# A third buffer for a pair's keys and values, and one normalising product a pair, in a kernel of attention and two expert layers

## The chip, the cores and the metric

The kernel runs on one core of a Trainium2 chip. The metric is the device time of one execution in microseconds, as the median of several runs. Beside the runs there is one profiled execution, from which all rows below come; its times count from the start of its span.

## The reference

Three layers follow each other. Only the first is touched by the change.

```python
# attention: 2 batches, 8 heads, 768 positions, 64 columns a head; 8 global keys, window of 96
scores = scale * np.matmul(q, k.transpose(0, 1, 3, 2))
is_global = pos[None, :] < n_global
is_local = (rel >= 0) & (rel < n_local)
keep = is_global | is_local
dist = np.where(is_global & ~is_local, n_local, np.abs(rel))
scores = scores - slopes[:, None, None] * dist
scores = np.where(keep, scores, -1e9)
a = np.exp(scores - np.max(scores, axis=-1, keepdims=True))
a = a / (np.sum(a, axis=-1, keepdims=True) + 1e-09)
x = np.matmul(a, v)                       # heads side by side: 1536 tokens x 512

# gated layer, 512 -> 1536 -> 512
xn = x / np.sqrt(np.mean(x * x, -1) + 1e-6) * rms_g
x = (silu(xn @ w_gate) * (xn @ w_val)) @ w_out

# 8 experts, each token goes to its best one
for e in range(8):
    out[mask_e] = gate[mask_e] * (np.maximum(x[mask_e] @ w1[e], 0) @ w2[e])
```

## The kernel before

The 1536 tokens are cut into six stages of two tiles of 128 (three stages a batch), and the heads into four pairs. A pair of heads in a stage is numbered 0 to 23 in the order of the work, four to a stage; one tile of 128 queries of such a pair is a unit, 0 to 47, so that pair 9 has the units 18 and 19. Because the window is shorter than a tile, a query tile needs its own key tile, the one before it and 32 columns of global keys.

`load_pair` (L200 on) brings a pair's keys, queries and values with DMAs of the SyncE queue. For the first eight pairs, called raw, keys and queries are used as they are, in float32: the matrix products of the scores (L533, L537, L538) read the loaded tiles `kn` and `qn` directly. For the later pairs `prep` splits them into a high and a low half: ScalarE writes the high half of the keys (L486, tile `kt`) and of the queries (L498, tile `qt`), GpSimd the low half of the keys (L489) and VectorE that of the queries (L499); the scores (L550) read `kt` and `qt`, so that `kn` and `qn` are free when these four have run. GpSimd also sets two columns of ones in the values' tile `vn` (L432), so that the product with the values gives the sums of the softmax as well, and copies windows of keys and values (L421, tiles `kt`, `vx`).

The first four pairs lie in tiles of their own (`duo`). From pair 4 on the three loaded tiles come from the pool `attn`, two buffers for each of `kn`, `qn` and `vn`. `prep(4)` and later ones also issue the loads of the pair two further on; `prep` of a pair stands in the code one pair ahead of its first unit, where the loop over units calls it.

A unit runs in three steps, `scores`, `turn` two units later and `values` three units after that. In `scores` TensorE writes the scores, VectorE adds the mask and takes the extreme (L557), ScalarE takes the exponential (L561). In `turn` TensorE transposes the probabilities into the PSUM banks `pt` (L572) and ScalarE copies them out (L580, tile `ptS`). In `values` TensorE multiplies them by the values (L601) into the one PSUM bank `xp`; after a pair's second tile VectorE takes the reciprocals of the sums (L608, L609) and scales both tiles into `duo` (L611).

When a stage's four pairs are done, `tail` normalises its rows and turns them (L387 to L404), and the gated layer can begin for it (`moe_block`, L769 on). In the first 60 us nothing else than attention and filling products (`warm`, L180) is there for TensorE; from then on products of the gated layer run between those of attention, until attention ends near 171 us. Weights of that layer are loaded and split at the same time (`convert64`, L334 to L354).

The order of instructions on each engine is drawn at build time by a planner: it has the program's order as priorities, a model of the durations, and the rule that a tile's buffer can be given out again when all readers of its last use are through. Each engine then runs its own list in order, and waits where it must. A change in the number of buffers therefore changes the list of every engine.

The lines of the loads ahead and of the buffers:

```python
nxt = range(NFP, NFP + 2) if gi == 0 else range(gi + 2, gi + 3) if gi >= NFP else ()
for gn in nxt:
    nat = [pool.tile([P, 2 * STAGE if x == "q" else 2 * DM if x == "k" else (ST_MAX + 1) * VW], F32, tag=f"{x}n", bufs=2, name=f"{x}n") for x in "kqv"]
    loaded.append(load_pair(*order[gn], *nat))
```

Of the kernel before, what the change touches and what calls it, by code (L numbers as in the profile page):

```python
# [8 lines left out]
F32 = mybir.dt.float32  # L9
# [5 lines left out]
ALU = mybir.AluOpType  # L15
# [4 lines left out]
P = 128  # L20
B, H, S, D = 2, 8, 768, 64
NT, DM, DFF = B * S, H * D, 1536
# [7 lines left out]
STARTS = [sum(SIZES[:i]) for i in range(len(SIZES))]  # L30
NSTAGE = len(SIZES)
ST = ST_MAX = max(SIZES)
STAGE = ST * P
TB = S // P
VW = 2 * (D + 1)
# [10 lines left out]
def kernel(  # L46
# [16 lines left out]
    nc = tc.nc  # L63
    slope = [2.0 ** (-(h + 1)) for h in range(H)]
    NFP, LATE = 4, 8
    NRAWG = 8
    XT = "ccccss"
    RING = "ccceewweec"
# [50 lines left out]
        out=nval, in0=nneg, scalar=4294967296.0, in1=nf[:, :, 0], op0=ALU.mult, op1=ALU.add  # L119
# [7 lines left out]
        out=flagf[:, 2:3], in0=nval[0:1, 1:2], scalar=float(LMAX), in1=flagf[:, 1:2], op0=ALU.is_le, op1=ALU.mult  # L127
# [11 lines left out]
        out=tri_f, in_=tri_f, pattern=[[1, P]], compare_op=ALU.is_gt, fill=0.0, base=0, channel_multiplier=-1  # L139
# [59 lines left out]
    def is_raw(st, hp):  # L199
        return st * NP + hp < NRAWG  # L200

    def load_pair(st, hp, kn, qn, vn):
        b, t0, nt = STARTS[st] // TB, STARTS[st] % TB, SIZES[st]
        i0 = 0 if t0 else 1
        nk = nt + 1 - i0
        k0 = (t0 - 1 + i0) * P
        hd = slice(P * hp, P * (hp + 1))
        if is_raw(st, hp):
            nc.sync.dma_start(out=kn[:, 0:nk * P], in_=kT[b][hd, k0:k0 + nk * P])
            nc.sync.dma_start(out=qn[:, 0:nt * P], in_=qT[b][hd, t0 * P:(t0 + nt) * P])  # L210
            nc.sync.dma_start(
                out=rows_of(vn)[:, i0:i0 + nk, 1:P + 1],
                in_=v[b, k0:k0 + nk * P, hd].rearrange("(t p) c -> p t c", p=P),
            )
            return kn, qn, vn
        for x, src in ((kn[:, 0:2 * nk * P], kT[b][hd, k0:k0 + nk * P]), (qn[:, 0:2 * nt * P], qT[b][hd, t0 * P:(t0 + nt) * P])):
            for r in range(2):
                nc.sync.dma_start(
                    out=x[D * r:D * (r + 1), :].rearrange("d (j s) -> d j s", j=2),
                    in_=src.rearrange("(j d) s -> d j s", j=2),  # L220
                )
        nc.sync.dma_start(
            out=rows_of(vn)[:, i0:i0 + nk, 1:P + 1],
            in_=v[b, k0:k0 + nk * P, hd].rearrange("(t p) c -> p t c", p=P),
        )
        return kn, qn, vn
# [7 lines left out]
    duo = [rp.tile([P, 2, DM], F32, name=f"duo{i}") for i in range(TT // 2)]  # L234
    part = [duo[i // 2][:, i % 2] for i in range(TT)]
# [54 lines left out]
    def body(is_fast):  # L290
# [9 lines left out]
        def ps(tag, bufs, name):  # L300
            return psum.tile([P, 512], F32, tag=tag, bufs=bufs, name=name)
# [108 lines left out]
        def fast_attention(pool):  # L410
            kg = pool.tile([P, NP, 2, GW], F32R, name="kg")

            kgr = pool.tile([P, NP, GW], F32, name="kgr") if NRAWG > NP else None
            kgn = pool.tile([P, NP, 2, GW], F32, name="kgn")
# [8 lines left out]
            def prep(gi):  # L423
                st, hp = order[gi]
                t0, nt = STARTS[st] % TB, SIZES[st]
                i0 = 0 if t0 else 1
                n = nt * P
# [6 lines left out]
                for gn in nxt:  # L434
                    if gn >= len(order):
                        break
                    nat = [
                        pool.tile([P, 2 * STAGE if x == "q" else 2 * DM if x == "k" else (ST_MAX + 1) * VW], F32, tag=f"{x}n", bufs=2, name=f"{x}n") for x in "kqv"
                    ]
                    loaded.append(load_pair(*order[gn], *nat))  # L440
                nk = nt + 1 - i0
                if gi == 0:
                    kg0 = kT[0].rearrange("(h d) s -> d h s", d=D)[:, :, 0:GW]
                    for r in range(2):
                        nc.sync.dma_start(
                            out=kgn[D * r:D * (r + 1)].rearrange("d a j s -> d (a j) s"), in_=kg0
# [3 lines left out]
                if gi == 2:  # L450
                    nc.scalar.activation(out=kg, in_=kgn, func=ACTF.Copy)
                    nc.gpsimd.tensor_tensor(
                        out=kg[D:P], in0=kgn[D:P], in1=kg[D:P].bitcast(F32), op=ALU.subtract
# [4 lines left out]
                f = 1 if t0 >= 2 else 3 - t0  # L458
# [34 lines left out]
                if hi_dve[1]:  # L493
                    nc.vector.tensor_scalar(
                        out=qhi, in0=srq, scalar1=0.125 / slope[2 * hp], scalar2=None, op0=ALU.mult
                    )
                else:
                    nc.scalar.activation(out=qhi, in_=srq, func=ACTF.Copy, scale=0.125 / slope[2 * hp])  # L498
                lo_eng[kq[1]].scalar_tensor_tensor(  # L499
                    out=qt[:, :, 1, 0:n], in0=srq, scalar=0.125 / slope[2 * hp], in1=qhi.bitcast(F32),  # L500
# [84 lines left out]
            def values(g, t, ptf, nb):  # L585
                st, t0, hp, qt, kt, vn, vx, mx = groups[g]
                nt = SIZES[st]
                if t == 0:
                    xps[g] = ps("x", 1, "xp")
                xp = xps[g]  # L590
                for j in range(2):
                    c = slice(j * (D + 1), (j + 1) * (D + 1))
                    o = xp[:, t * VW + j * (D + 1):t * VW + (j + 1) * (D + 1)]
                    for a in range(nb):
                        if nb == 1 or a == 1:
                            rhs = vn[:, t + 1, c]
                        elif t0 + t == 1:
                            rhs = vn[:, t, c]
                        else:
                            rhs = vx[:, t, c]  # L600
                        nc.tensor.matmul(  # L601
                            out=o, lhsT=ptf[:, (j * nb + a) * P:(j * nb + a + 1) * P], rhs=rhs,
                            start=(a == 0), stop=(a == nb - 1),
                        )
                if t == nt - 1:
                    rc = pool.tile([P, ST, 2], F32, tag="rc", bufs=2, name="rc")
                    xs3 = xp[:, 0:nt * VW].rearrange("p (t c) -> p t c", c=VW)
                    nc.vector.tensor_scalar(out=rc[:, 0:nt], in0=xs3[:, :, 0:VW:VW - 1], scalar1=1e-9, scalar2=None, op0=ALU.add)  # L608
                    nc.vector.reciprocal(rc[:, 0:nt], rc[:, 0:nt])  # L609
                    for tt in range(nt):  # L610
                        nc.vector.tensor_tensor(  # L611
                            out=part[STARTS[st] + tt][:, hp * P:(hp + 1) * P].rearrange("p (j d) -> p j d", j=2),
                            in0=xp[:, tt * VW + 1:tt * VW + 1 + P].rearrange("p (j d) -> p j d", j=2),
                            in1=rc[:, tt].unsqueeze(2).to_broadcast([P, 2, D]), op=ALU.mult,
                        )
                    groups[g] = None

            warm(WARM1)
            prep(0)
            yield "work"  # L620
            tails = []
            q1, q2 = [], []
            n = hold = 0
            while n < len(units) or q1 or q2:
# [18 lines left out]
                if last is not None:  # L643
                    g, t = last
                    if t == SIZES[g // NP] - 1 and g % NP == NP - 1:
                        st = g // NP
# [518 lines left out]
        while True:  # L1165
# [12 lines left out]
            while True:  # L1178
                if moe is None and ready:
                    st = ready.pop(0)  # L1180
# [45 lines left out]
        for a in range(KD):  # L1226
            raw = rp.tile([P, P, NE], F32, tag="raw", bufs=NRAW, name="rawg")
            nc.sync.dma_start(out=raw, in_=r_gate[a * P:(a + 1) * P, :].partition_broadcast(P))
            for h in range(2):
                nc.scalar.activation(  # L1230
                    out=rgb[h][:, :, a * P:(a + 1) * P],
# [34 lines left out]
        st, ms = NSTAGE - 1, range(M1, NM)  # L1266
        prep_next(0, first, len(first))
        banks["mm"] = MMC.split()
        with tc.manual_schedule(engines={mybir.EngineType.PE}):
# [10 lines left out]
            x = expert_tile(w1t[0], w2t[0], tka, wta, xsa, lambda: None, True)  # L1280
# [21 lines left out]
        for e in range(NE):  # L1302
# [17 lines left out]
            if e == 0:  # L1320
                x = expert_tile(w1t.pop(0), w2t.pop(0), tks[:, 0:1], wts[:, 0:1], xs.pop(0), between)
# [58 lines left out]
```

## Time and profile before

| what | value |
|---|---|
| median of 3 runs | 655.97 us (655.12 to 656.81) |
| the profiled execution's own time | 655.69 us |
| its span | 654.0 us |
| mean granted TensorE clock | 0.988 |
| TensorE busy | 628.9 us, 96% |
| VectorE busy | 446.2 us, 68% |
| ScalarE busy | 320.3 us, 49% |
| GpSimd busy | 208.7 us, 32% |
| moved by DMA | 82.98 MB, 127 GB/s on average |

The profile calls the engines PE (TensorE's products), PEld (its weight loads), DVE (VectorE), ACT (ScalarE), POOL (GpSimd) and SP (SyncE; SPq is its queue). Products on TensorE are pipelined and their ends are modelled, so that "busy" says that it is supplied and not that it is at its peak. A wait is put down to what came last. A row of the order of time merges neighbours of the same kind and gives start, duration, engine, line, operation, output and inputs, count, and in brackets the idle time before it with its releaser.

### The profile page before, as it was taken

To read this page: it belongs to the slowest core of one execution; us is meant where nothing else is said; L and a number is where in the kernel's file an instruction comes from. 1 tells how busy PE (TensorE), PEld (TensorE's weight loads), DVE (VectorE), ACT (ScalarE), POOL (GpSimd) and SP (SyncE) were. 2 spreads that over 40 slices of the span, in tenths; PEclk is the share of its full clock that TensorE was granted. 3 is DMA by queue.
4 is the path that set the end of the run, shared out by engine and by line. 5 is a ranking of instruction groups with operands and counts; after the bars stand their busy time and mean duration, and the time that the engine had idled before them with its cause. 6 is when DMAs were issued, how large, how long until landed. Compare 5 with 4: busy or idle time off the path is not lost. (4 is left out here: it accounts for less than half of the span.)

```text
span 654.0 us, 11691 instructions
## 1 busy us (share of the span) xinstructions
PE 628.9 (96%) x4280; PEld 562.3 (86%) x4281; DVE 446.2 (68%) x1098; ACT 320.3 (49%) x624; POOL 208.7 (32%) x275
## 2 busy tenths in 40 slices
PE   9998998899999999999999999999999999999992
PEld 4667887899999999999999999997888899899891
DVE  5765888976599988676359998944667464664410
ACT  3666798777555533334622221333656564654420
POOL 4415758663122212111222532461610221011010
PEclk9999899899999999999999999999999999999997
DMA  7536466551044532131311010442978667454000
GB/s 228 158 90 201 127 174 181 157 149 39 1 130 130 161 98 72 59 98 65 129 65 65 2 65 34 122 138 82 301 261 261 206 217 253 168 189 140 17 13 30
DMA packets 56567, 82.98 MB, mean 127 GB/s; under 512 B 7983, under 2 KB 38703, under 8 KB 56496
## 3 DMA queue, kind: packets, MB, share of 16 engines
q1 hardware_dynamic: 53552, 74.75, 36.9%
q0 software_dynamic: 2944, 7.35, 3.4%
q8 instruction: 37, 0.61, 0.4%
q14 instruction: 34, 0.28, 0.1%
HBM read 75.75 MB, written 7.39 MB: 127 GB/s over the span
## 5 line engine op out<-in xcount | busy, mean ns | idle before, releaser
L769 PE MATMUL pg<-xn,gv 128*128 128x256 f32 x1728 | 228.2, 285 | 1.2 <-DVE th L778 1.2
L769 PEld LDWEIGHTS pg<-xn,gv 128*128 128x128 f32 x1728 | 220.2, 192 | 8.2 <-DVE th L778 1.5
L787 POOL TENSOR_TENSOR hid<-hf,hid 128x256 fp32r<-128x256 f32 x72 | 61.4, 855 | 174.6 <-ACT hid L786 174.5
L806 PE MATMUL po<-ow,hid 128*128 128x512 f32 x432 | 113.9, 394 | 0.0
L1017 PE MATMUL py<-ew,eh 128*128 128x512 f32 x384 | 91.2, 395 | 0.9 <-DVE eh L1084 0.5
L1017 PEld LDWEIGHTS py<-ew,eh 128*128 128x128 f32 x384 | 71.3, 188 | 17.7 <-DVE eh L1084 0.9
L806 PEld LDWEIGHTS po<-ow,hid 128*128 128x128 f32 x432 | 75.5, 189 | 11.7 <-POOL hid L787 0.3
L1039 PE MATMUL ph<-xs,ew 128*128 128x256 f32 x672 | 83.1, 283 | 0.0
L1039 PEld LDWEIGHTS ph<-xs,ew 128*128 128x128 f32 x672 | 81.6, 191 | 0.7
L786 ACT ACTIVATE hid<-hf 128x256 fp32r<-128x256 f32 x72 | 29.9, 417 | 83.7 <-DVE hf L782 81.9
L1024 POOL DMA_INDIRECT out_dram<-yo,tk x16 | 16.5, 1034 | 139.1 <-ACT yo L1023 107.7
L838 DVE CUSTOM_DVE_ANT_0 jk<-duo,rgb 128x512 bf16<-128x512 f32 x64 | 54.3, 849 | 0.5
L561 ACT ACTIVATE pr<-pr,mx 128x256 f32<-128x256 f32 (+1 forms) x96 | 45.1, 484 | 14.0 <-DVE mx L557 13.2
L957 DVE TENSOR_TENSOR ew<-rawe,ew 128x1024 fp32r<-128x1024 f32 (+1 forms) x36 | 40.8, 1134 | 12.9 <-ACT ew L953 12.9
L1048 DVE SCALAR_TENSOR_TENSOR eh<-ph,eh 128x256 fp32r<-128x256 f32 x56 | 23.1, 423 | 37.5 <-ACT eh L1047 35.5
L777 ACT ACTIVATE th<-pg 128x256 f32<-128x256 f32 x72 | 27.2, 379 | 39.8 <-PE pg L769 37.3
L957 DVE TENSOR_TENSOR ew<-duo,ew 128x1024 fp32r<-128x1024 f32 x28 | 34.1, 1224 | 17.9 <-ACT ew L953 16.8
L953 ACT ACTIVATE ew<-rawe 128x1024 fp32r<-128x1024 f32 x36 | 38.0, 1059 | 10.2 <-PE pg L769 4.6
L778 DVE SCALAR_TENSOR_TENSOR th<-th,pg 128x256 f32<-128x256 f32 x72 | 29.7, 415 | 16.4 <-ACT th L777 15.4
L1047 ACT ACTIVATE eh<-ph 128x256 fp32r<-128x256 f32 x56 | 21.2, 384 | 39.2 <-PE ph L1039 38.1
L953 ACT ACTIVATE ew<-duo 128x1024 fp32r<-128x1024 f32 x28 | 29.4, 1059 | 19.4 <-PE py L1017 19.4
L815 DVE TENSOR_TENSOR duo<-duo,po 128x512 f32<-128x512 f32 x36 | 23.4, 684 | 18.7 <-PE po L806 18.6
(178 smaller groups left out, 935.8 us busy)
## 6 DMA issues: line engine op xcount, KB each, us to landing
rawe<-in_moe_w_dram SPq DMA_DIRECT2D x36, 512.0 KB, 5.0
duo<-in_moe_w_dram SPq DMA_DIRECT2D x28, 512.0 KB, 5.4
raw<-in_moe_w_gate_dram SPq DMA_DIRECT2D x12, 512.0 KB, 3.8
raw<-in_moe_w_val_dram SPq DMA_DIRECT2D x12, 512.0 KB, 5.6
raw<-in_moe_w_out_dram SPq DMA_DIRECT2D x12, 512.0 KB, 3.4
kn<-in_k_dram SPq DMA_DIRECT2D x28, 192.0 KB, 3.3
qn<-in_q_dram SPq DMA_DIRECT2D x36, 128.0 KB, 2.9
vn<-in_v_dram SPq DMA_DIRECT2D x16, 192.0 KB, 2.6
```

Of the source, the lines that this page charges most:

```text
L561: pin["act"] = nc.scalar.activation(out=pr[:, j, 0:n], in_=pr[:, j, 0:n], func=ACTF.Exp, bias=mx[:, t, j:j + 1], scale=-1.0,)
L769: nc.tensor.matmul(out=pg[:, 0:n_], lhsT=gv[:, i, a, kk, :], rhs=x[st][:, kk, :], start=(n == 0), stop=(n == 3 * KD - 1),)
L777: pin["th"] = nc.scalar.activation(out=th, in_=pss[0][:, 0:n_], func=ACTF.Tanh, scale=0.5)
L778: nc.vector.scalar_tensor_tensor(out=th, in0=th, scalar=1.0, in1=pss[0][:, 0:n_], op0=ALU.add, op1=ALU.mult)
L786: nc.scalar.activation(out=hh[:, 0], in_=hf, func=ACTF.Copy)
L787: nc.gpsimd.tensor_tensor(out=hh[:, 1], in0=hf, in1=hh[:, 0].bitcast(F32), op=ALU.subtract)
L806: nc.tensor.matmul(out=po, lhsT=hid[mi][:, a, t * P:(t + 1) * P], rhs=ow[:, c, :], start=(mi == 0 and n == 0), stop=(mi == len(ms) - 1 and ...
L838: nc.vector.tensor_tensor_reduce(out=jk, in0=part[i0 + t], in1=rgb[e // 4][:, e % 4, :], scale=1.0, scalar=0.0, op0=ALU.mult, op1=ALU.add, ...
L953: cp = nc.scalar.activation(out=t[:, 0], in_=raw, func=ACTF.Copy)
L957: nc.vector.tensor_tensor(out=t[:, 1, 0:nd], in0=raw[:, 0:nd], in1=t[:, 0, 0:nd].bitcast(F32), op=ALU.subtract)
L1017: last_mm["py"] = nc.tensor.matmul(out=py, lhsT=hid(m, a, j), rhs=w2t[m // 2][:, c, (m % 2) * DM:(m % 2 + 1) * DM], start=(n == 0), stop=( ...
L1039: nc.tensor.matmul(out=ph[:, 0:CAP], lhsT=w1t[kk][:, a, m * P:(m + 1) * P], rhs=x[:, kk, :], start=(n == 0), stop=(n == 3 * KD - 1),)
```

## The change

The pool's tiles of keys and values get three buffers each, those of queries keep two. The tile of keys is cut from 1024 to 768 columns, which is what a pair needs at most. The product that scales both tiles of a pair by the reciprocals of their sums becomes one instruction over both tiles instead of one for each.

```diff
+    NKN, NQN, NVN = 3, 2, 3
...
                     nat = [
-                        pool.tile([P, 2 * STAGE if x == "q" else 2 * DM if x == "k" else (ST_MAX + 1) * VW], F32, tag=f"{x}n", bufs=2, name=f"{x}n") for x in "kqv"
+                        pool.tile([P, w], F32, tag=f"{x}n", bufs=nb, name=f"{x}n")
+                        for x, w, nb in (
+                            ("k", 2 * (ST_MAX + 1) * P, NKN), ("q", 2 * STAGE, NQN), ("v", (ST_MAX + 1) * VW, NVN)
+                        )
                     ]
...
-                    for tt in range(nt):
-                        nc.vector.tensor_tensor(
-                            out=part[STARTS[st] + tt][:, hp * P:(hp + 1) * P].rearrange("p (j d) -> p j d", j=2),
-                            in0=xp[:, tt * VW + 1:tt * VW + 1 + P].rearrange("p (j d) -> p j d", j=2),
-                            in1=rc[:, tt].unsqueeze(2).to_broadcast([P, 2, D]), op=ALU.mult,
-                        )
+                    nc.vector.tensor_tensor(
+                        out=duo[st][:, :, hp * P:(hp + 1) * P].rearrange("p t (j d) -> p t j d", j=2),
+                        in0=xs3[:, :, 1:P + 1].rearrange("p t (j d) -> p t j d", j=2),
+                        in1=rc[:, 0:nt].unsqueeze(3).to_broadcast([P, nt, 2, D]), op=ALU.mult,
+                    )
```

## Rows read from the trace of the kernel before

**Rows 1.** Page, busy time of the engines (TensorE and its weight loads).
```profile
PE 628.9 (96%) x4280; PEld 562.3 (86%) x4281; DVE 446.2 (68%) x1098; ACT 320.3 (49%) x624; POOL 208.7 (32%) x275
```
**Rows 2.** Stages: length, busy time by engine, granted clock, DMA share, GB/s.
```profile
31.00:56.00 25.00, 25.00 (x155) 17.73 (x154) 16.07 (x58) 15.37 (x32) 9.45 (x12) 1.00 0.49 148
...
61.80:64.10 2.30, 0.11 (x2) 0.09 (x2) 0.00 (x0) 1.86 (x4) 0.88 (x1) 1.00 0.92 232
64.10:70.00 5.90, 5.90 (x39) 5.90 (x40) 4.17 (x7) 5.51 (x13) 4.94 (x8) 0.71 0.61 151
...
110.00:120.00 10.00, 6.40 (x52) 5.85 (x52) 9.19 (x22) 8.62 (x17) 7.23 (x11) 1.00 0.61 159
120.00:125.00 5.00, 5.00 (x29) 4.87 (x29) 5.00 (x15) 2.29 (x5) 4.24 (x5) 0.66 0.66 189
125.00:180.00 55.00, 55.00 (x442) 53.15 (x441) 36.27 (x117) 39.12 (x86) 23.74 (x40) 1.00 0.25 70
```
**Rows 3.** The same columns for one microsecond.
```profile
66.00:67.00 1.00, 1.00 (x7) 1.00 (x7) 0.38 (x2) 0.93 (x3) 0.88 (x3) 0.50 0.53 91
```
**Rows 4.** Waits of TensorE, 56 to 131 us: total, times, longest.
```profile
PE sp L550 <- DVE mx L557: 4.6, 7, 1.4
PE pp L572 <- ACT ptS L580: 2.2, 1, 2.2
```
**Rows 5.** ScalarE in order of time: start, duration, operation, idle before it.
```profile
62.24 0.84 ACT L486 ACTIVATE kt<-kn 128x768 fp32r<-128x768 f32 x1 [2.43 <-DMA kn<-in_k_dram]
...
66.60 1.15 ACT L498 ACTIVATE qt<-qn 128x512 fp32r<-128x512 f32 x2
```
**Rows 6.** SyncE's queue in order of time, loads of keys and queries.
```profile
49.68 1.28 SPq L218 DMA_DIRECT2D kn<-in_k_dram  x2
...
57.07 0.60 SPq L218 DMA_DIRECT2D qn<-in_q_dram  x1
57.86 2.97 SPq L218 DMA_DIRECT2D kn<-in_k_dram  x4
...
61.51 2.71 SPq L218 DMA_DIRECT2D qn<-in_q_dram  x3
```
**Rows 7.** TensorE in order of time.
```profile
56.31 0.64 PE L538 MATMUL sp<-kn,qn 64*128 64x224 f32 x4
...
64.02 0.44 PE L572 MATMUL pp<-ident,pr 128*128 128x128 f32 x2 [2.19 <-ACT ptS L580]
...
70.16 0.40 PE L550 MATMUL sp<-kt,qt 128*128 128x256 f32 x2
```
**Rows 8.** Page, DMA issues: count, size, microseconds from issue to landing.
```profile
qn<-in_q_dram SPq DMA_DIRECT2D x36, 128.0 KB, 2.9
```
**Rows 9.** Waits of GpSimd, 60 to 131 us.
```profile
POOL vn L432 <- DMA vn<-in_v_dram: 7.1, 7, 2.3
```
**Rows 10.** VectorE in order of time: two products with masked scores between them.
```profile
85.15 0.29 DVE L611 TENSOR_TENSOR duo<-xp,rc 128x128 f32<-128x128 f32 x1
85.36 0.41 DVE L557 CUSTOM_DVE_ANT_0 pr<-sp,half 128x256 f32<-128x256 f32 x1
...
85.70 0.28 DVE L611 TENSOR_TENSOR duo<-xp,rc 128x128 f32<-128x128 f32 x1
```
**Rows 11.** Groups of VectorE, 60 to 131 us: count, busy, mean ns, idle before.
```profile
L499 DVE SCALAR_TENSOR_TENSOR qt<-qn,qt 128x512 fp32r<-128x512 f32 x12 | 15.9, 1330 | 1.6 <-ACT qt L498 1.6
...
L611 DVE TENSOR_TENSOR duo<-xp,rc 128x128 f32<-128x128 f32 x20 | 5.0, 286 | 0.2
```
**Rows 12.** VectorE in order of time, after the idle time at 61.6 us.
```profile
64.88 0.69 DVE L404 TENSOR_TENSOR xn<-trx,xn 128x512 fp32r<-128x512 f32 x1 [3.31 <-ACT xn L403]
```
**Rows 13.** Line L499: shortest, median and longest in ns.
```profile
L499 DVE SCALAR_TENSOR_TENSOR qt<-qn,qt x16: 680/1051/2272, 55.9 to 148.2; 128x512 fp32r<-128x512 f32 x16
```
**Rows 14.** VectorE and GpSimd in order of time, one pair's low halves.
```profile
76.34 1.85 DVE L499 SCALAR_TENSOR_TENSOR qt<-qn,qt 128x512 fp32r<-128x512 f32 x1
...
75.81 1.83 POOL L489 TENSOR_TENSOR kt<-kn,kt 64x768 fp32r<-64x768 f32 x1 [0.68 <-POOL kt L421]
```

## The prediction, made before the changed kernel was run

> **What bounds the kernel now.** I read the engine totals first. TensorE is busy 628.9 us of the 654.0 us span [rows 1], so only time that it loses can be won back. A table by stage then says where it loses any: in 31 to 56 us it is busy 25.00 of 25.00 us, from 125 to 180 us 55.00 of 55.00 us, but in 61.8 to 64.1 us only 0.11 of 2.30, and in 110 to 120 us 6.40 of 10 [rows 2]. [...]
>
> The waits of TensorE in 56 to 131 us name the releasers: 2.2 us in one piece for ScalarE's copy of turned probabilities (L580), and 4.6 us in seven pieces for VectorE's masked scores (L557) [rows 4]. The first is the one that this change can touch. I followed it back through four views. ScalarE's own order: it idles 2.43 us until 62.24 us for a DMA of keys, to start the conversion at L486, and behind that conversion in its queue stand the exponentials and the copy that TensorE waits for [rows 5]. SyncE's queue: keys are issued at 49.68 us (two halves) and then not until 57.86 us (four halves), with one half of queries at 57.07 us [rows 6]. TensorE: the last raw scores that read the keys and queries of pair 7 start at 56.31 us [rows 7]. So the keys of pair 9 had to wait for the slot of pair 7: with two buffers, pair 9 takes the slot of pair 7, and raw pairs hold their keys until their scores are done. The same chain then delays unit 18, the first of pair 9: its scores come at 70.16 us [rows 7].
>
> In the second hole VectorE is nearly full, 9.19 of 10 us [rows 2], and there as in most of 70 to 125 us TensorE's holes are VectorE's doing [rows 4].
>
> **The change part by part.** *Third buffer for the keys.* Pair 9 now takes the slot of pair 6. Pair 8 took that slot at 49.68 us [rows 6], so it is free from about then; the keys of pair 9 can land before 55 us, and ScalarE's conversion of them has nothing to wait for at 59.8 us. This removes the 2.19 us hole [rows 7] and, with the hole gone, the low clock behind it: (1 - 0.71) x 5.90 us = 1.7 us of full-speed time [rows 2]. Bounds: 0 to 2.2 us for the hole, 0 to 1.7 us for the clock. I take both whole, since the next thing due is earlier than the hole's end. That next thing is the queries of pair 9, which keep two buffers and still need pair 7's slot. Their first half was issued at 57.07 us [rows 6]; with the second 0.65 us behind it and a landing time of 2.9 us [rows 8] they are there at 60.6 us, 1.6 us before the keys came until now. ScalarE can use them then or later; TensorE had work until 61.8 us anyway. Loads of pairs 6 to 8 also move earlier, in or ahead of a stretch in which TensorE runs without a gap [rows 2], so this brings nothing. What it can cost is DMA queueing alone, which I put at nothing: SyncE issues the same number of loads, none is larger, and the keys of a later pair come behind those that are used sooner.
>
> *Third buffer for the values.* GpSimd's clearing of the two sum columns (L432) waits 7.1 us, in seven pieces, for loads of values in 60 to 131 us [rows 9]. In its queue behind that clearing stand the low halves of keys (L489) and the window copies. Yet no wait of TensorE of any size is put down to GpSimd in that stretch [rows 4]. I take 0 for the end; the bounds are a gain of 1.0 us, from work of GpSimd that comes earlier, and a loss that is the rival on collisions below. On SyncE's queue the loads of values now stand further ahead; a load behind them is held for less time, not more.
>
> *One product instead of two.* The two products go to 24 merged ones. Alone, a 128x128 product starts at 85.15 us and the next instruction of VectorE at 85.36: it holds the engine for 0.21 us. A 128x256 instruction that also reads PSUM starts at 85.36 us and the next full one at 85.70: 0.34 us [rows 10]. So a merged pair costs 0.34 instead of 0.42, about 0.07 us less. In 60 to 131 us, the stretch in which VectorE sets the pace, there are 20 products [rows 11], ten pairs: 10 x 0.07 = 0.7 us. Elsewhere it is covered. Bounds: 0, and 0.21 us a pair if the second came free, 2.1 us; the start-to-start rows are the nearest, so 0.7. The one extra dimension of the pattern and the single accumulator bank (one buffer) change nothing that I can see: the bank is given back 0.07 us sooner.
>
> [...]
>
> *Memory.* Keys take 3 x 768 instead of 2 x 1024 columns, values 3 x 390 instead of 2 x 390: 1.0 and 1.5 KB more a partition, no time.
>
> **The sum.** 2.2 + 1.7 + 0.7 = 4.6 us. As a cross-check from the other engine: VectorE's order holds 3.31 us of idle time at 61.6 to 64.9 us, caused by the same hold of ScalarE [rows 12]; that is time which the engine that sets the pace afterwards gets back, and with 0.7 us of lighter products it is 4.0. The profiled execution took 655.69 us, its span is 654.0, so 1.69 us lie around it; the median of the runs is 655.97, 0.28 us above that execution. Profile: 654.0 - 4.6 = 649.4, and 651.1 with what lies around it. On the median: 655.97 - 4.6 = 651.4 us.
>
> **The rivals.** *Queries in the place of keys (same).* The second half of the queries went at 61.51 us, behind four halves of keys [rows 6]. With three key buffers even more keys are free to go at 57 us. If it stays where it is, it lands at 61.51 + 2.9 = 64.4 us, and if ScalarE's conversion of queries (L498) is queued ahead of the exponentials, the hole is 64.4 - 62.24 = 2.2 us longer and the clock falls as before: 655.97 + 2.2 - 0.7 = 657.5. If ScalarE is held only as long as now, it is 655.3. For it: the queries keep two buffers, and the whole order is drawn anew by the planner. Against it: that conversion stands at 66.60 us now, far behind the exponentials [rows 5]. Middle 656.4.
>
> *The change does nothing where it matters.* If the load is issued late for another reason (SyncE's own order), the time stays at 655 to 656. Against it speaks that the first load for pair 9 left at 57.07 us, 0.1 us after the raw scores of pair 7 ended (56.31 + 0.64) [rows 6, 7]: the slot held it, not the queue.
>
> *Collisions of VectorE and GpSimd (slower).* The query residual at L499 takes 0.68 us at its shortest and 2.27 at its longest [rows 13]. One that starts at 76.34 us takes 1.85 us while GpSimd's L489 runs from 75.81 for 1.83 us [rows 14]. It ends 0.55 us after GpSimd does, so it was held until GpSimd had finished. The 12 of 60 to 131 us take 15.9 us [rows 11], where 12 x 0.68 would be 8.2. If GpSimd, no longer stopped by the values, runs L489 beside all of them, they take 12 x 1.85 = 22.2 us, 6.3 more, on the engine that sets the pace. Past four more collisions (4.6 / 1.17) the gain is eaten; with all, and one more fall of the clock (1.7 us), the time is 655.97 - 4.6 + 6.3 + 1.7 = 659.4. Against it: GpSimd's work does not grow, it only moves, and some of its waits end now just where VectorE begins. [...]
>
> *The second hole goes too (faster still).* In 110 to 120 us TensorE idles 3.6 us and the clock then costs (1 - 0.66) x 5 = 1.7 us [rows 2]. If VectorE comes to this place with less of a backlog, up to 5.3 us more go: 646.1 to 649.5.
>
> **How the numbers follow.** Forecast 0.48, its own range 649.5 to 653.5. Queries in place of keys 0.22 (655.3 to 657.5). No effect 0.05. Collisions 0.15 (657.9 to 659.4 and a little over). Second hole 0.10 (646.1 to 649.5). A difference of 0.3%, 2.0 us, is about what a measurement can tell from none. Faster by more: 0.48 + 0.10 = 0.58. Within: 0.22 + 0.05 = 0.27. Slower: 0.15. The range 647.5 to 657.9 leaves out the collisions and the lower half of the last case, 0.20.
>
> **What would show it.** Right: loads of keys of pair 9 issued near 50 us, no wait of ScalarE for keys near 60 us, no idle piece of TensorE of 2 us there and a granted clock of 1.00 in 64 to 70 us; unit 18's scores before 65 us; 24 products of about 0.42 us. Wrong: a wait of ScalarE for queries in the same place, or L499 above 1.33 us on average in the stretch after it. The weakest step is that the order of instructions around 60 us stays what it is. It is drawn anew when a buffer is added, and the seven small holes of 70 to 120 us can come out larger or smaller with it.

## The result, and the profile after

| | median, us | runs | span of the profiled execution, us | mean granted clock |
|---|---|---|---|---|
| before | 656.39 | 655.05 to 657.65 | 654.0 | 0.988 |
| changed | 663.65 | 663.29 to 668.37 | 661.8 | 0.977 |

The changed kernel takes 1.0115 times the time of before, 95% interval 1.009 to 1.0141: it is 7.3 us slower by the medians and 7.5 by the ratio, where 4.6 us less were forecast. (Single executions far above the others, 678 to 692 us and once 3482 us, occur with several kernels here, the one before included, and are left out of all ratios, though not of the medians.)

The same views, now of the changed kernel; behind the diff a line number is 1 to 4 higher (in the experiments up to 7). First the engine totals of the page, which answer [rows 1].

```profile
PE 634.4 (96%) x4280; PEld 566.4 (86%) x4281; DVE 442.5 (67%) x1074; ACT 318.9 (48%) x624; POOL 215.2 (33%) x275
```

TensorE is busy 5.5 us longer with the same 4280 records. Products do take longer at the low clock: those of L772 have a mean of 427 ns in 84.65 to 91.4 us, at 0.50, and of 296 ns in 61 to 84 us, at 1.00. The table by stage (columns as in [rows 2]) shows where.

```profile
45.00:50.50 5.50, 4.20 (x28) 2.66 (x28) 5.16 (x13) 3.14 (x7) 3.94 (x7) 1.00 0.64 193
50.50:60.80 10.30, 10.30 (x40) 7.94 (x39) 2.79 (x11) 3.52 (x7) 4.01 (x6) 0.50 0.68 186
61.80:64.10 2.30, 2.30 (x22) 1.83 (x22) 0.78 (x4) 1.51 (x4) 1.71 (x1) 1.00 0.14 15
64.10:70.00 5.90, 5.90 (x49) 5.51 (x49) 4.56 (x19) 4.25 (x9) 3.94 (x6) 1.00 0.84 217
78.00:84.00 6.00, 3.54 (x26) 2.79 (x24) 5.97 (x16) 3.71 (x10) 4.10 (x6) 1.00 0.36 101
84.50:91.50 7.00, 7.00 (x35) 7.00 (x35) 3.71 (x11) 4.04 (x10) 4.61 (x8) 0.51 0.60 171
```

The third and fourth lines are what was forecast: the hole of 61.8 to 64.1 us is gone and the clock behind it is 1.00, where [rows 2] have 0.11 us of 2.30 and 0.71. The other lines are new. TensorE idles 1.30 us in 45 to 50.5 us and then runs 10.3 us at 0.50; it idles 2.46 us in 78 to 84 us and then runs 7 us at 0.51. ScalarE in order of time shows how the first of these begins, and one line of before stands below it for comparison.

```profile
47.37 0.84 ACT L490 ACTIVATE kt<-kn 128x768 fp32r<-128x768 f32 x1 [2.27 <-DMA kn<-in_k_dram]
48.12 0.61 ACT L354 ACTIVATE gv<-cv 128x512 fp32r<-128x512 f32 x1
48.64 0.49 ACT L565 ACTIVATE pr<-pr,mx 128x256 f32<-128x256 f32 x1
```

Before, the same conversion:

```profile
53.70 0.84 ACT L486 ACTIVATE kt<-kn 128x768 fp32r<-128x768 f32 x1 [0.86 <-DMA kn<-in_k_dram]
```

TensorE's piece that follows from it, and SyncE's loads of keys (these answer [rows 6]):

```profile
49.19 0.44 PE L576 MATMUL pp<-ident,pr 128*128 128x128 f32 x2 [1.30 <-ACT pr L565]
```

```profile
43.09 1.29 SPq L219 DMA_DIRECT2D kn<-in_k_dram  x2
...
50.19 0.60 SPq L219 DMA_DIRECT2D kn<-in_k_dram  x1
...
52.19 0.60 SPq L219 DMA_DIRECT2D kn<-in_k_dram  x1
```

The third buffer did not only let pair 9's keys go at 50 to 52 us instead of 57.86 us. It also let pair 8's go at 43.09 instead of 49.68 us, and the planner, which lays out each engine's list by its own estimate of when data arrive, put their conversion 6.3 us earlier into ScalarE's list, ahead of exponentials. ScalarE then waits 2.27 us for the transfer; the first exponential behind it had its input, VectorE's masked scores, at 46.7 us and starts at 48.64. It is the hold of [rows 5], one pair earlier.

The whole attention and the stretch at 440 to 480 us, in which the first two experts begin, first for the changed kernel, then for the one before:

```profile
0.00:200.00 200.00, 188.87 (x1283) 159.84 (x1285) 142.09 (x434) 129.80 (x284) 100.34 (x164) 0.95 0.48 131
440.00:480.00 40.00, 36.96 (x205) 29.27 (x204) 18.28 (x49) 16.82 (x26) 22.28 (x19) 1.00 0.49 166
```

```profile
0.00:200.00 200.00, 189.51 (x1322) 161.06 (x1324) 150.42 (x470) 134.99 (x291) 99.47 (x166) 0.98 0.48 136
440.00:480.00 40.00, 38.40 (x215) 30.81 (x214) 21.49 (x49) 19.22 (x30) 14.11 (x13) 1.00 0.64 216
```

TensorE's idle time up to 200 us hardly grows, from 10.5 to 11.1 us. The time lost at the low clock, (1 - clock) summed over one-microsecond windows, goes from 3.4 to 10.2 us, and 440 to 480 us has 1.4 us more of idle time. Together this is 8.8 us more; the span grew by 7.8.

### The profile page after: what moved, and what is told of

It reads as the page before. It is cut to its first block, busy times and chain, and to the rows that moved or that the text cites. A ratio compares the mean times of both kernels' runs of the same rounds, so it can differ in the third digit from the quotient of the medians.

```text
span 661.8 us, 11652 instructions
## 1 busy us (share of the span) xinstructions
PE 634.4 (96%) x4280; PEld 566.4 (86%) x4281; DVE 442.5 (67%) x1074; ACT 318.9 (48%) x624; POOL 215.2 (33%) x275
## 5 line engine op out<-in xcount | busy, mean ns | idle before, releaser
L772 PE MATMUL pg<-xn,gv 128*128 128x256 f32 x1728 | 228.7, 284 | 0.0
L772 PEld LDWEIGHTS pg<-xn,gv 128*128 128x128 f32 x1728 | 219.6, 191 | 6.1
L809 PEld LDWEIGHTS po<-ow,hid 128*128 128x128 f32 x432 | 75.7, 188 | 12.6 <-POOL hid L790 0.5
L565 ACT ACTIVATE pr<-pr,mx 128x256 f32<-128x256 f32 (+1 forms) x96 | 45.1, 485 | 22.6 <-DVE mx L561 22.4
L956 ACT ACTIVATE ew<-rawe 128x1024 fp32r<-128x1024 f32 x36 | 38.0, 1058 | 10.2 <-PE pg L772 4.7
```

Of the source, the lines that this page charges most:

```text
L565: pin["act"] = nc.scalar.activation(out=pr[:, j, 0:n], in_=pr[:, j, 0:n], func=ACTF.Exp, bias=mx[:, t, j:j + 1], scale=-1.0,)
L772: nc.tensor.matmul(out=pg[:, 0:n_], lhsT=gv[:, i, a, kk, :], rhs=x[st][:, kk, :], start=(n == 0), stop=(n == 3 * KD - 1),)
L809: nc.tensor.matmul(out=po, lhsT=hid[mi][:, a, t * P:(t + 1) * P], rhs=ow[:, c, :], start=(mi == 0 and n == 0), stop=(mi == len(ms) - 1 and ...
L956: cp = nc.scalar.activation(out=t[:, 0], in_=raw, func=ACTF.Copy)
```

## The experiments

The first four runs were set against three theories. A: the early conversion of pair 8's keys is the cause. B: the single product has the order drawn anew, and that is the cause. C: collisions between VectorE and GpSimd, the slower rival of the prediction. Each result is the median of its executions, then the ratio to the kernel before on the same chip with its 95% interval.

**e1, the product alone.** Two buffers of each kind, one product per pair.

```diff
-    NKN, NQN, NVN = 3, 2, 3
+    NKN, NQN, NVN = 2, 2, 2
```

> Only the merged product; two buffers for keys and values as before (the tile of keys cut to 768 columns). Theory A (the third buffer for keys lets the planner put pair 8's key conversion at L490 ahead of the exponentials on ScalarE, ScalarE then waits for the load, TensorE stands still near 48 us and its clock stays low for 10 us): no such wait at 45 to 50 us, time within 2 us of the kernel before, 654 to 657.5. Theory B (the merged product, which draws the order of every engine anew, is the cause): 661 to 665. Theory C (collisions of VectorE and GpSimd after the values come earlier): as A here.

660.78 us, 1.0065 (1.0048 to 1.0081).

**e2, the key buffer alone** (3, 2, 2 and the two products of before).

> Only the third buffer for keys; two products and two buffers for values. Theory A: ScalarE waits some 2 us for keys near 45 to 48 us, TensorE idles over 1 us there, the granted clock is 0.50 for several us after it, and the first scores of pair 8 come at 62 us or later against 58.57 before; time 659 to 664. Theory B: no such hole, 654 to 657.5. Theory C: as B, since the values are unchanged.

659.69 us, 1.0043 (1.0024 to 1.0062).

**e3, the value buffer alone** (2, 2, 3 and two products).

> Only the third buffer for values. Theory A: the keys of pair 8 leave at 49 to 50 us as before, no hole before 60 us, time 654 to 657.5. Theory C: L499 goes above 1.33 us on average in 60 to 131 us and the time rises by 3 us or more, 659 to 664.

664.14 us, 1.0091 (1.0053 to 1.013). So each part alone is slower, and the three do not add up to the whole. A cannot be the sole cause: e1 and e3 have no third key buffer, and in e2 the mark of A is missing, for ScalarE does wait 1.53 us for keys until 48.59 us, but no wait of TensorE follows there. B cannot be the sole cause either, since e2 and e3 keep the two products. Against C speaks that the query residual takes 1186 ns on average in 60 to 131 us of e3, less than the 1330 of before [rows 11]. What the key buffer does is nevertheless seen. TensorE's piece for ScalarE's copy [rows 7] stays where there are two key buffers, in e1 and, in the second fence, e3:

```profile
64.65 0.53 PE L576 MATMUL pp<-ident,pr 128*128 128x128 f32 x2 [2.19 <-ACT ptS L584]
```

```profile
63.26 1.11 PE L401 MATMUL trx<-ident,duo 128*128 128x128 f32 x4 [2.12 <-ACT ptS L584]
```

It goes in e2, whose stages are these, with the longest wait of TensorE in the second:

```profile
60.00:70.00 10.00, 9.72 (x84) 9.39 (x83) 6.24 (x24) 7.63 (x17) 4.85 (x8) 1.00 0.63 170
70.00:80.00 10.00, 7.15 (x58) 6.42 (x56) 9.20 (x23) 6.40 (x16) 6.78 (x9) 0.93 0.29 89
78.50:89.00 10.50, 9.03 (x44) 8.72 (x43) 5.45 (x21) 5.36 (x13) 5.72 (x10) 0.51 0.61 185
```

```profile
77.22 0.50 PE L554 MATMUL sp<-kt,qt 128*128 128x256 f32 x2 [1.83 <-DVE mx L561]
```

60 to 70 us is nearly full (9.72 of 10) and at 1.00. Ten microseconds later TensorE idles 2.85 us, and 10.5 us at 0.51 follow: (1 - 0.51) x 10.5 = 5.1 us, more than the 3.9 that went.

**e4, conversions held back** in the changed kernel, each put behind the last exponential (L565) that was written ahead of it.

```diff
-                    nc.scalar.activation(out=ks, in_=src, func=ACTF.Copy)
+                    ka = nc.scalar.activation(out=ks, in_=src, func=ACTF.Copy)
+                    if pin["act"] is not None:
+                        behind(ka, pin["act"])
...
-                    nc.scalar.activation(out=qhi, in_=srq, func=ACTF.Copy, scale=0.125 / slope[2 * hp])
+                    qa = nc.scalar.activation(out=qhi, in_=srq, func=ACTF.Copy, scale=0.125 / slope[2 * hp])
+                    if pin["act"] is not None:
+                        behind(qa, pin["act"])
```

> The whole change, and in addition the conversions of keys and queries on ScalarE may not be put ahead of the exponential that was traced last before them. Loads and buffers stay as in the changed kernel. Theory A: the hole at 48 us and the low clock from 50 to 61 us go, the first scores of pair 8 come near 58.5 us instead of 64.1, time 652 to 658. If the loss comes from the loads themselves, from the values or from the product, the time stays at 661 to 665.

683.35 us, 1.0411 (1.0388 to 1.0435). The pin is a dependence like any other, so the whole list is drawn anew and the attention falls behind (1132 products of TensorE up to 200 us, 1322 before):

```profile
0.00:200.00 200.00, 178.08 (x1132) 147.07 (x1134) 129.65 (x397) 118.05 (x257) 92.27 (x159) 0.90 0.43 123
```

That experiment does not test A cleanly. What the four share is a new order. **Theory D:** the loss is the new order's, and the buffers and the product cost next to nothing by themselves.

To test D, I took the order out of the planner's hands. A kernel can carry the list of another: each instruction gets an order-only dependence on the one that stands ahead of it in that list, on its own engine (the few instructions of the overflow branch at the end stay free). `made` holds the instructions as they were written, ORDER their positions in the order wanted, one engine after the other with -1 between.

```diff
+            prev = -1
+            for k in struct.unpack("<%dh" % 6018, zlib.decompress(base64.b85decode(ORDER))):
+                if k >= 0 and prev >= 0:
+                    tc.add_manual_dep(
+                        made[k], made[prev].name,
+                        mybir.DependencyInfo(mybir.DependencyClass.NoSync, mybir.DependencyReason.DATA), reason="order",
+                    )
+                prev = k
```

**e5, the whole change in the order of before.** The 24 second products drop out of VectorE's list; nothing else in the lists differs.

> The whole change (three key buffers, three value buffers, one product per pair), with every engine held to the order of instructions of the kernel before: each instruction gets an order-only dependence on the one that stands ahead of it in that list, and the second product's place falls away. Theory D (the loss is the planner's new order, the buffers and the product cost nothing by themselves): 654.5 to 657.0 us, scores of u16 at 58.6 +/- 0.5, last product of the attention at 170.9 +/- 1, two low-clock stretches of 1.7 us lost each, as before. Theory C (the third buffers' places or the wider product cost time through collisions): 659 to 664 us, in this order too.

655.39 us against 657.11 of before on that chip, 0.9978 (0.9954 to 1.0003). The whole loss is gone. Three marks in the trace were missed: unit 16's scores come at 59.49 us, attention ends near 167 us, and there is no low clock up to 200 us where two stretches were expected.

**e7, the order of e1 on the kernel before:** two buffers, two products, not one operation changed.

> The kernel before, nothing changed in its buffers or instructions (two products per pair), but held to the order of instructions that the planner drew for the run with the merged product alone (second product right behind the first). Theory D: 659.5 to 661.5 us, as that run, with its holes and its three low-clock stretches. If the loss of that run was the merged product's own: 654.5 to 657 us.

662.61 us, 1.0077 (1.0045 to 1.0108). That is e1's loss without e1's edit, a little above the range expected. The list carries its waits along: TensorE's pieces of 2.19, 0.77, 1.62 and 2.77 us in e1 (64.65, 78.79, 97.23, 124.28 us) stand in e7 as 2.54, 0.83, 1.68 and 2.82 us (63.65, 79.00, 97.50, 125.64 us), for the same releasers. The last of them, in e1 and then in e7:

```profile
124.28 0.47 PE L554 MATMUL sp<-kt,qt 128*128 128x256 f32 x2 [2.77 <-DVE mx L561]
```

```profile
125.64 0.47 PE L553 MATMUL sp<-kt,qt 128*128 128x256 f32 x2 [2.82 <-DVE mx L560]
```

**e8, the two products of a pair in reverse order**, an edit that changes no work, left to the planner.

```diff
-                    for tt in range(nt):
+                    for tt in reversed(range(nt)):
```

> The kernel before with the two normalising products of a pair written in reverse order (second tile first): same work, same buffers, same operations; the planner draws the order anew. Theory D: the time moves by more than the measurement's 2 us although nothing was added, to 657.5 to 664 us (the other three redraws gave 659.7 to 664.1), with new low-clock stretches. If a redraw is harmless: 655 to 657.5 us.

661.29 us, 1.0074 (1.0053 to 1.0096). Three runs from three sides: D holds. The lines of 0 to 200 us for e5, e7 and e8, one fence each:

```profile
0.00:200.00 200.00, 190.40 (x1342) 161.07 (x1344) 149.93 (x451) 135.73 (x293) 100.01 (x166) 1.00 0.51 139
```

```profile
0.00:200.00 200.00, 187.39 (x1286) 159.23 (x1288) 145.32 (x459) 129.80 (x284) 98.10 (x164) 0.96 0.46 131
```

```profile
0.00:200.00 200.00, 189.06 (x1291) 158.34 (x1293) 141.84 (x461) 131.49 (x286) 96.94 (x164) 0.97 0.48 133
```

**e6, as e5, and pair 9's two key transfers one place further ahead on SyncE**, in front of pair 9's first query transfer. This is the forecast's mechanism and nothing else.

> As the run before it (the whole change in the old order), and the two transfers of pair 9's keys stand one place further ahead on SyncE's queue, in front of pair 9's first query transfer (which waits for a buffer until about 57): this is what the prediction took the third key buffer to do, and nothing else moves. The prediction's mechanism: ScalarE's wait for the keys at 62 goes, TensorE's hole of 2.2 us at 61.8 to 64.0 goes and so does the low clock behind it (1.7): 651 to 653 us, scores of u18 before 68. First rival (the queries or another input are late next): 655 to 657 us, the hole stays at 1.5 us or more. Second rival (the hole goes, but the low clock comes in another place): 653 to 655 us.

654.18 us, 0.9952 (0.9923 to 0.9981). The stretch is as forecast (first two lines), and the next thing is late (third line, ScalarE, TensorE):

```profile
61.80:64.10 2.30, 2.30 (x24) 2.30 (x23) 1.62 (x6) 2.23 (x5) 2.21 (x4) 1.00 0.87 214
64.10:70.00 5.90, 5.90 (x53) 5.90 (x53) 3.16 (x8) 4.40 (x12) 4.19 (x8) 1.00 0.54 134
77.75:84.75 7.00, 6.99 (x35) 6.49 (x34) 5.89 (x18) 5.39 (x13) 4.29 (x7) 0.51 0.61 186
```

```profile
66.51 1.15 ACT L505 ACTIVATE qt<-qn 128x512 fp32r<-128x512 f32 x2 [1.50 <-DMA qn<-in_q_dram]
...
74.73 0.63 ACT L505 ACTIVATE qt<-qn 128x512 fp32r<-128x512 f32 x1 [1.54 <-DMA qn<-in_q_dram]
...
470.79 1.06 ACT L959 ACTIVATE ew<-rawe 128x1024 fp32r<-128x1024 f32 x1 [2.21 <-DMA rawe<-in_moe_w_dram]
471.76 1.04 ACT L959 ACTIVATE ew<-duo 128x1024 fp32r<-128x1024 f32 x1
472.70 0.58 ACT L1078 ACTIVATE hr<-ph 128x512 f32<-128x512 f32 x1
```

```profile
75.81 0.44 PE L579 MATMUL pp<-ident,pr 128*128 128x128 f32 x2 [1.42 <-ACT pr L568]
...
473.33 0.66 PE L1085 MATMUL trh<-ident,hr 128*128 128x128 f32 x4 [1.71 <-ACT hr L1078]
```

Of the cases expected for this run it is the last: the hole goes and the low clock comes elsewhere. What is late is what the prediction's first rival named, queries in the place of keys. Pair 9's own hold ScalarE for 1.50 us until 66.51 us, with no wait of TensorE behind them; two pairs on, ScalarE stands at pair 11's queries (which keep two buffers), TensorE waits 1.42 us for the exponential behind them, and the low clock follows. Another part is given back far behind the attention. In e5 and e6 the work at 470 us comes some 2 us earlier, meets a weight transfer that has not landed, and ScalarE's eviction of hidden rows, which had its input, stands behind that conversion.

**e9, as e6, with two instructions moved in ScalarE's list:** pair 11's query conversion two places back, the eviction of hidden rows two places forward. (From here on the expectations read D more narrowly: time is lost where an in-order engine waits for a transfer with ready work behind it.)

> The run with pair 9's keys early, with two more instructions moved in ScalarE's list and nothing else: pair 11's query conversion (in that run it waits 1.54 us for its transfer at 74.73, TensorE then 1.42 us for the exponential behind it, and the low clock follows at 77.8 to 84.8, 3.4 us lost) goes behind the exponential and the eviction that stand after it; and the second half of the first expert's hidden rows goes ahead of two weight conversions (the first waits 2.21 us for its transfer at 470.79, TensorE then 1.71 us at 473.33). Theory D (time is lost where an in-order engine waits for a transfer with work behind it that has its inputs, and more of it in the low clock behind the hole): both holes go, the low clock at 78 to 85 goes, 648.5 to 652 us. Rival (the transfers, busy 0.92 at 460 to 480, set the pace, a moved wait only comes back): 653 to 655 us, with the same sum of idle time and low clock in other places.

652.67 us, 0.9937 (0.9915 to 0.9958). In its profiled execution the clock stood low for 65 us (last section), so **e12** ran the same kernel once more, for a profile that can be set beside the others.

> The kernel of the run with two more holes out, once more, for a profile at the clock that the others had. Theory D: 650.5 to 653.5 us; no wait of TensorE over 1 us at 55 to 90 and at 460 to 480, u24 near 82, last product near 165. Rival (the gain is of other origin, the holes stand elsewhere): the time as before, but waits of TensorE of 3 us or more in sum at 55 to 130 beyond those on VectorE's maxima.

653.91 us, 0.9959 (0.9937 to 0.998). Both medians lie above the range expected under D, by 0.7 and 0.4 us, and what the two moves add to e6 (0.9952) can't be told. This one line is all that the view of TensorE's waits has for 55 to 90 us; below it are the two stretches:

```profile
PE sp L557 <- DVE mx L564: 2.0, 4, 0.8
```

```profile
0.00:200.00 200.00, 191.85 (x1356) 162.75 (x1358) 151.37 (x456) 137.35 (x297) 99.35 (x167) 1.00 0.51 139
440.00:480.00 40.00, 37.40 (x212) 30.29 (x212) 22.91 (x50) 20.67 (x32) 15.99 (x12) 1.00 0.64 213
```

No low clock is left up to 200 us, and the idle time there is 8.2 us. The span is 650.2 us, 3.8 less than before. At 440 to 480 us only part is won back: the pieces of 1.71 and 0.78 us have become one of 0.35, but 1.3 us at another eviction stand there now (2.60 us in all, 3.13 in e6). The rival is right by that much.

**e10 and e13: are the buffers needed at all?** Both are the kernel before, two buffers and two products, in its own order. In e10 ScalarE's conversion of pair 9's keys goes behind the two exponentials and the eviction that stood after it. In e13 three conversions go back: pair 9's keys, pair 10's keys, pair 11's queries.

> The kernel before, two buffers and two products, in its own order, with one instruction moved: ScalarE's conversion of pair 9's keys (it waits 2.43 us for the transfer at 62.24) goes behind the two exponentials and the eviction that stand after it. If the third key buffer was needed to take that hole away: the hole only moves, 655 to 657 us. If the order on ScalarE alone does it (theory D): no hole over 1 us at 61 to 64, no low clock at 65 to 69, 651.5 to 654 us; between these ends if part is given back at 440 to 480 as in the two runs in the old order.

655.82 us, 0.9981 (0.9962 to 1.0). In time order on ScalarE and on TensorE:

```profile
63.48 0.84 ACT L489 ACTIVATE kt<-kn 128x768 fp32r<-128x768 f32 x1 [1.58 <-DMA kn<-in_k_dram]
64.23 0.58 ACT L406 ACTIVATE xn<-trx 128x512 fp32r<-128x512 f32 x1
```

```profile
64.86 3.02 PE L772 MATMUL pg<-xn,gv 128*128 128x256 f32 x20 [1.16 <-ACT xn L406]
```

The 2.19 us hole has become one of 1.16 us for the next instruction in line, others follow at 70 and 78 us, and the time is within 0.3% of before.

> The kernel before (two buffers, two products, its own order), with three of ScalarE's conversions moved back: pair 9's keys behind two exponentials and the two evictions that stood after them, pair 10's keys behind two exponentials, pair 11's queries behind one exponential and one eviction. Theory D without any need of a third buffer: 651.5 to 654 us, no wait of TensorE over 1.2 us at 55 to 90. If the early transfers (which the third key buffer allows) are needed: 655 to 657 us, because the keys come late for the scores themselves and TensorE then waits on the converted keys.

657.14 us, 1.0013 (0.9998 to 1.0029). TensorE now waits for GpSimd's copies. Their chain can't start before pair 9's keys are converted; it starts at 63.62 us, behind a conversion that got its transfer at 62.64 us:

```profile
67.58 0.47 PE L553 MATMUL sp<-kt,qt 128*128 128x256 f32 x2 [1.04 <-POOL vx L424]
...
70.77 0.44 PE L604 MATMUL xp<-vx,ptS 128*128 128x65 f32 x2 [1.53 <-POOL vx L424]
```

With two buffers the data themselves are late. In these runs a gain came only with both: the early transfer, which the third key buffer allows (e6, 0.9952, beside e13, 1.0013; e10's interval overlaps e6's), and a list that does not spend it (e6 beside e2, 1.0043).

**e11, three buffers of each kind, two products, the order of before.**

> Three key and three value buffers with two products per pair, every engine held to the order of the kernel before. Theory D: 654.5 to 657 us; in that order no transfer starts earlier by more than a microsecond, so the third buffers neither give nor take. If this run's attention ends with the last product near 168 (as with the whole change in the old order), the buffers gave the 2.9 us there; if near 170.9, the single product did, by the prediction 0.7 us of it and the rest by low clock that stays away.

654.68 us, 0.9977 (0.9947 to 1.0007); last product at 172.8 us. Beside e5's 0.9978 this says that the single product is worth nothing that can be told here. The last product does not decide it: e11 has the list of before, yet 3.4 us of low clock at 64.75 to 71.75 us where before has 1.7, so such stretches differ even where the list is the same.

The accounts of the profiled executions (e9's is left to the last section), in us: idle time of TensorE and time lost at the low clock up to 200 us, idle time at 440 to 480 us (40 less the busy time), and span.

| | idle | low clock | idle 440 to 480 | span |
|---|---|---|---|---|
| before | 10.5 | 3.4 | 1.6 | 654.0 |
| changed | 11.1 | 10.2 | 3.0 | 661.8 |
| e1, e2, e3 | 12.5, 11.3, 11.3 | 5.1, 5.1, 10.2 | 3.1, 2.3, 1.0 | 659.1, 659.0, 662.5 |
| e4 | 21.9 | 20.5 | 0.4 | 681.4 |
| e5, e6, e12 | 9.6, 7.6, 8.2 | 0, 3.4, 0 | 3.3, 3.1, 2.6 | 654.0, 653.6, 650.2 |
| e7, e8 | 12.6, 10.9 | 8.5, 5.1 | 2.5, 1.6 | 660.1, 659.0 |
| e10, e11, e13 | 10.4, 9.3, 11.4 | 5.1, 5.1, 0 | 1.8, 1.7, 1.0 | 655.4, 655.8, 653.6 |

e5, e6 and e13 lose another 1.7 us each at the low clock in 440 to 460 us. The columns are no full account: from before to e8 they grow by 2.1 us, the span by 5.0, and where the rest lies stays open.

## Why the prediction was wrong, step by step

**The step that failed** is the one that the prediction named as its weakest and then priced at nothing: that the order of instructions around 60 us stays. It says itself that the order is drawn anew when a buffer is added, yet its sum has no term for that, and of the earlier loads it says "What it can cost is DMA queueing alone, which I put at nothing". Of the rivals only the one on queries leans on a new order, at 657.5 us at most. Five edits left to the planner (changed, e1, e2, e3, e8) were all slower, by 0.43 to 1.15%, and e4 with its pins by 4.1%; the same change with the order held was not (e5). The price of a redraw was to be had only from such runs: 4.9 us (0.74%) for e8, which changes no work, and 2.8 to 7.5 us for the five, beside a forecast gain of 4.6.

**"Loads of pairs 6 to 8 also move earlier", and "this brings nothing".** The second half was wrong. They move earlier, and the planner moves their consumers with them, ahead of work that is ready. A stretch without a gap [rows 2] is not one that can't get one.

**The third key buffer, hole and clock (3.9 us).** The mechanism was right. In the changed kernel pair 9's keys go at 50 us, ScalarE has no such wait near 60 us, and 61.8 to 70 us is full at clock 1.00; e6 shows it with nothing else moved. One mark failed for the reason above: unit 18's scores come at 68.47 us, not before 65. The size was too large: "the next thing due is earlier than the hole's end" was argued for pair 9's queries, with 60.6 us for their arrival. In e6 they come at 66.51 us and unit 18's scores at 67.66 us; that costs TensorE no wait, but pair 11's queries do. Nor was the low clock sure to be won: in e5, where pair 9's keys are as late as before, the piece is 1.59 us and no low clock follows it.

```profile
64.00 0.44 PE L579 MATMUL pp<-ident,pr 128*128 128x128 f32 x2 [1.59 <-ACT ptS L587]
```

From e5 to e6 the ratio falls from 0.9978 to 0.9952, and the intervals overlap. With two more holes out it is 0.9937 and 0.9959, which is 4.1 and 2.7 us of 656.6: the forecast's 4.6 us (0.70%) lies in the first interval and outside the second.

**The single product (0.7 us).** The 24 products take 405 to 425 ns, as forecast; in 60 to 131 us the groups of VectorE that answer [rows 11] are

```profile
L503 DVE SCALAR_TENSOR_TENSOR qt<-qn,qt 128x512 fp32r<-128x512 f32 x11 | 12.8, 1159 | 4.9 <-ACT qt L502 4.9
...
L614 DVE TENSOR_TENSOR duo<-xp,rc 128x256 f32<-128x256 f32 x10 | 4.2, 418 | 0.1
```

One takes 418 ns where two took 572 [rows 11], 0.154 us less busy time a pair. Over 24 pairs that is 3.7 us, and VectorE's total did fall by as much (446.2 to 442.5 us); but it fell to 440.9 us in e8 too, which keeps both products, so the total proves nothing. Nor is busy time what the engine gains, for the next instruction starts before the record of the last one ends:

```profile
47.95 0.41 DVE L614 TENSOR_TENSOR duo<-xp,rc 128x256 f32<-128x256 f32 x1
48.28 0.41 DVE L561 CUSTOM_DVE_ANT_0 pr<-sp,tabG 128x256 f32<-128x256 f32 x1
```

From start to start the product holds VectorE for 0.33 us here, and for 0.33 to 0.35 us in most places where the engine does not wait: the 0.34 us of the prediction, so that its term was sized about right (0.42 - 0.34 is 0.08 us a pair, where it wrote 0.07). At the end of the kernel nothing of it can be told (e5 beside e11).

**The values' buffer (0).** That is what e11 shows within its interval. GpSimd's wait for values [rows 9] did not even shrink in the changed kernel, where the order was new: 14.8 us in six pieces instead of 7.1 in seven.

**Collisions, the slower rival.** They did not grow. The query residual takes 1159 ns on average in the stretch, less than before [rows 11], and with the order held the same buffers and the same product cost nothing (e5). That rival had the right sign for the wrong reason: its 657.9 to 659.4 us stood for collisions, not for the order. **No effect** and **the second hole** did not happen either: in the changed kernel TensorE still waits 1.65 us until 125.13 us, and the clock costs 1.7 us behind it.

**What stays open.** Why five redraws of five are worse than the order of before is not explained by one cause: TensorE's new pieces have releasers on ScalarE, VectorE and GpSimd. That the changed kernel's loss begins with the early conversion of pair 8's keys was read from its trace; taking away that conversion's place alone was not tried, and e2, where the same keys go early too, has no wait of TensorE there. Whether the order of before is a lucky draw among many can't be told from five others.

## What to carry to other kernels

Where a planner draws the order, an edit's price is its own effect plus a redraw. Measure the redraw with an edit that does nothing, and measure the edit with the old order held. An earlier transfer helped here only where the instruction that waits for it did not move ahead of ready work in an in-order list. After each hole that goes, look at once for the next input that is late. Give the low clock behind a hole its own line in the sum, with nothing as its lower bound.

## What the runs showed of the hardware

The low clock behind a hole cost more than the hole in several of these runs, and the hole's length did not tell how much. A piece of 1.30 us (changed, 49.19 us) was followed by 10.3 us at 0.50, one of 1.42 us (e6, 75.81 us) by 7.0 us at 0.51, and one of 2.19 us (before [rows 7]) by 3.75 us (65.25 to 69.0, in windows of a quarter microsecond); in e13 pieces of 1.04 and 1.53 us had no low clock behind them. Even at one place of nearly the same list it differs: behind pair 9's keys 2.19 us (before) were followed by a loss of 1.7 us, 2.25 us (e11) by 3.4 us, and 1.59 us (e5) by none. In the profiled execution of e9 the clock stood at 0.50 for 65 us, while TensorE was busy all the time (65.25 of 65.25 us); the last wait ahead of it was 1.94 us.

```profile
22.38 0.44 PE L579 MATMUL pp<-ident,pr 128*128 128x128 f32 x2 [1.94 <-ACT pr L568]
```

```profile
24.25:89.50 65.25, 65.25 (x224) 43.67 (x223) 25.28 (x83) 25.09 (x51) 12.88 (x17) 0.50 0.29 87
```

By that account (1 - 0.50) x 65.25 = 32.6 us went in one stretch.
